# A fused retention and ELU feed-forward kernel on one core: w_out brought in by converting transfers on GpSimd's queue, and the second group's first matrix product cut in two halves

## The chip, the cores and the metric

The kernel runs on one core of a Trainium2 chip. The core has a tensor engine (TensorE, PE in the profile, with PEld for its weight loads), a vector engine (VectorE, DVE), a scalar engine (ScalarE, ACT), GpSimd (POOL) and a sync engine (SyncE, SP), which here only issues transfers. Each engine runs its own list of instructions in order, and they wait for each other by semaphores. Transfers between the chip's main memory and the core's working memory run on sixteen DMA engines, whichever engine issued them; those issued by SP and those issued by GpSimd stand in two different queues (q1 and q0 in the profile). The metric is the device time of one execution in microseconds, and the number given for a kernel is the median of several executions.

## The reference

Inputs and output are float32. The first part is a retention (attention with a decay in place of the softmax), the second a feed-forward network with an ELU between two matrix products.

```python
# q, k, v: [8 batches, 8 heads, 576 tokens, 64]; w_in: [512, 2048]; w_out: [2048, 512]
scores = (1 / sqrt(64)) * q @ k.transpose(0, 1, 3, 2)
gamma  = 1 - 2 ** (-5 - arange(8))                       # one decay for each head
Dmat   = where(rel >= 0, gamma ** rel, 0)                # rel = query position - key position
attn   = (scores * Dmat) @ v
x      = attn, heads side by side: [4608 tokens, 512]
h      = x @ w_in
g      = where(h > 0, h, exp(min(h, 0)) - 1)             # ELU
out    = g @ w_out                                       # [4608, 512]
```

## The kernel before

**Units.** The retention is cut into units, listed in `seq` (L161 to L166). A unit of a batch is a half `T` of its first 512 tokens (256 tokens) and a half `w` of the heads (four), so a batch has four such units, and one tail unit for its last 64 tokens with all heads. Units 0 to 3 are batch 0, units 4 to 7 batch 1, units 8 and 9 the tails of batches 0 and 1, units 10 to 13 batch 2, unit 14 its tail, and so on. The decay is a power of the position, so it is folded into q and k while they are converted to bf16 (`cast_qk`, L192): two instructions for q, two for k, one for v (`cast_v`). Then q and k are turned, either by a transposing transfer issued by SP (`turn`, L233) or on TensorE with a copy back by VectorE or ScalarE (`turn_pe`, L238). `stretch(u)` (L409) is the work of a unit on TensorE: the part of unit u-1 that comes from earlier tokens (`inter`), the scores of u, the masked scores of u-1 times v (`values`), and the running state of u (`state`). VectorE adds the state up (`prefix_mid`, `prefix_end`), and GpSimd copies it into block form for TensorE (`put_mid`, `put_end`, L403 and L406, two instructions each). `puts` does both copies, and `finish(u)` is the last half of a stretch alone. `put_x` lays the result down as the bf16 columns of the feed-forward input.

**Feed-forward.** The 4608 tokens make nine groups: group g below 8 is the first 512 tokens of batch g, and group 8 (`B` in the code, tiles `xtail` and `gt`) is the eight tails. For a group, `ffn1(g, ft)` (L460) is block ft of sixteen of the first product: four matmuls into a PSUM tile `ph`, an exponential and a relu on ScalarE, and one instruction on VectorE that makes the bf16 tile `g`. `ffn2(g, it, fts)` (L501) adds blocks of the second product for 128 tokens into `pm`; after block 15, ScalarE copies the result and GpSimd issues the store at the next `flush`. With `nf=2` and 256 columns, `ffn1` puts two blocks of half the tokens into one PSUM tile (used for group 8, `f1t`). There are three PSUM banks with the tag `ph`, one with `pm`, two for scores and two (`x0`, `x1`) for the retention's sums; the first group borrows the last two for some of its `ph` tiles (L649).

**Weights.** w_in and w_out come as float32 in sixteen pairs of 128-row blocks (`load_w(k)`, L150): eight pairs of w_in and eight of w_out, 256 KB a transfer, two transfers a pair, issued by SP into the ring of float32 tiles `rqk` (ten tiles), which the units' q and k use as well (`load`, L174). `cast_w(k)` (L155) converts a pair to bf16, two instructions on GpSimd. Block ft of the first product needs a quarter of w_in (two pairs), and row ft of the second product needs one block of w_out.

**Order.** Every instruction is pinned to the order in which the code issues it (`pin`). The order of the first third is written out by hand: loads of units 0 to 3 and of six weight pairs, the retention of batch 0 (L532 to L597), then group 0's two products woven with the remaining weight conversions and with units 4 to 7 (L632 to L709, where `one(ft, r)` is one block of the first product and row r of the second for the first two `it`). SP's list there is: pairs 4, 5, 10, 11, unit 4, pairs 6, 7, 12, 13, unit 5, pairs 14, 15, units 6, 7, 8, 10, 9. From L748 on, `stage(jobs, upto)` spreads unit steps evenly over feed-forward jobs. A step (L602) loads four units ahead, converts and turns two units ahead, and does the stretch of its own unit, so seven steps lie in the first stage (units 8 to 14) and five in most others.

## Time and profile before

| | |
|---|---|
| three runs | 317.7, 319.59 and 319.09 us, median 319.09 |
| the profiled execution's own time | 321.6 us |
| its span | 319.9 us |
| busy share of the span | PE 95%, ACT 66%, POOL 54%, DVE 52% |
| transfers | 54.00 MB, of them 8.92 MB in GpSimd's queue (q0), 44.58 MB in SP's (q1) |

How to read it: a time in a view is counted from the start of the span. A group of instructions carries the line of the code that made it, the engine, and the output and inputs by the program's names. "[1.50 <-DMA qkT<-qkn]" behind an instruction says how long its engine sat idle before it and what ended that. All matmuls have the line of the helper `mm` (L65), so they are told apart by their tiles. In the table by stretches of time, each row has the busy time of every engine, the clock that TensorE was granted (1.00 is full), the busy share of the sixteen DMA engines (which can exceed 1, since packets overlap) and the bytes per time that they moved.

### The profile page before, as it was taken

How to read it: one execution, taken by the hardware profiler on the slowest of the kernel's cores; microseconds unless marked ns; L12 is line 12 of the kernel's file. 1: busy time of each engine (PE TensorE's matmuls, PEld its weight loads, DVE VectorE, ACT ScalarE, POOL GpSimd, SP SyncE). 2: the span in 40 equal slices, each digit the busy share in tenths (PEclk: the TensorE clock that was granted, in tenths of full speed). 3: DMA queues.
4: the chain of work that ended last, by engine and by line, in shares of the span. 5: the costliest groups of instructions: out<-in, count | busy, mean ns of one | idle time of the engine just before them, and what ended most of it. 6: DMA issues, size and time to landing. Idle time of an engine off the chain costs nothing.

```text
span 319.9 us, 7923 instructions
## 1 busy us (share of the span) xinstructions
PE 304.4 (95%) x3104; PEld 158.1 (49%) x3104; DVE 166.8 (52%) x309; ACT 212.1 (66%) x417; POOL 173.9 (54%) x380
## 2 busy tenths in 40 slices
PE   8889698997999999999999999999999999999994
PEld 5544344543554544554444675545454544456541
DVE  5755557267756765654445564665456543434400
ACT  3678455576777886777677777677777777677511
POOL 5889867896697775646354555555965200001010
PEclk9799979999999999999999999999999999999998
DMA  7999999499999997658366464764943000000112
GB/s 214 316 329 360 355 290 242 126 261 224 204 232 279 252 214 210 170 148 181 102 164 174 142 166 118 164 182 133 216 99 85 35 33 33 35 33 34 60 74 66
DMA packets 100774, 54.00 MB, mean 169 GB/s; under 512 B 45056, under 2 KB 94208, under 8 KB 100736
## 3 DMA queue, kind: packets, MB, share of 16 engines
q1 hardware_dynamic: 97984, 44.58, 58.2%
q0 software_dynamic: 2752, 8.92, 7.8%
q8 instruction: 24, 0.39, 0.5%
q14 instruction: 14, 0.11, 0.1%
HBM read 36.70 MB, written 9.44 MB: 144 GB/s over the span
## 4 chain that ended last, share of the span: by engine, by line
PE 79%; POOL 7%; DMA 7%; ACT 2%; DVE 1%; issue 1%; SPq 1%; ACTq 0%; POOLq 0%
PE pm L65 36%; PE ph L65 34%; PE x L65 5%; PE sc L65 4%; DMA rqk<-in_k_dram 3%; POOL qkn L197 3%; DMA qkT<-qkn 2%; DMA rqk<-in_moe_w_in_dram 2%; POOL w_in_sb L158 2%; ACT e L470 1%; PE ptr L246 1%; POOL w_out_sb L158 1%; DVE g L481 1%; SPq L186 1%; POOL s_mid L401 0%
## 5 line engine op out<-in xcount | busy, mean ns | idle before, releaser
L481 DVE SCALAR_TENSOR_TENSOR g<-e,ph 128x512 bf16<-128x512 f32 x128 | 87.5, 686 | 106.4 <-ACT ph L474 106.2
L65 PE MATMUL ph<-xt,w_in_sb 128*128 128x512 bf16 x512 | 131.8, 382 | 1.8 <-DVE g L481 0.9
L65 PE MATMUL pm<-w_out_sb,g 128*128 128x512 bf16 x512 | 131.9, 380 | 0.7 <-POOL w_out_sb L158 0.4
L470 ACT ACTIVATE e<-ph 128x512 f32<-128x512 f32 x144 | 85.9, 596 | 57.2 <-PE ph L65 57.1
L65 PEld LDWEIGHTS <-w_in_sb 128*128 128x128 bf16 x640 | 60.3, 98 | 63.2 <-issue 3.8
L474 ACT ACTIVATE ph<-ph 128x512 f32<-128x512 f32 x144 | 85.2, 594 | 0.0
L65 PEld LDWEIGHTS <-g 128*128 128x128 bf16 x512 | 49.4, 98 | 57.0 <-issue 1.7
L518 POOL DMA_DIRECT2D out_dram<-ot x36 | 20.5, 570 | 82.3 <-ACT ot L509 75.6
L401 POOL CAST s_mid<-mid 64x128 bf16<-64x128 f32 x64 | 18.6, 291 | 41.9 <-DVE mid L385 21.2
L197 POOL TENSOR_TENSOR qkn<-rqk,gk 128x256 bf16<-128x256 f32 x64 | 38.0, 614 | 4.7 <-DMA rqk<-in_k_dram 4.5
L304 DVE TENSOR_TENSOR pt<-sc,mask 128x1024 bf16<-128x1024 f32 x31 | 37.8, 1218 | 3.1 <-PE sc L65 3.1
L359 ACT CAST xt<-x 128x256 bf16<-128x256 f32 x62 | 23.5, 450 | 15.8 <-PE x L65 15.6
L509 ACT COPY ot<-pm 128x512 f32<-128x512 f32 x36 | 20.9, 587 | 19.4 <-PE pm L65 19.4
L197 POOL TENSOR_TENSOR qkn<-rqk,gq 128x256 bf16<-128x256 f32 x50 | 29.6, 612 | 1.6 <-DMA rqk<-in_q_dram 0.2
L481 DVE SCALAR_TENSOR_TENSOR gt<-e,ph 128x256 bf16<-128x256 f32 x32 | 12.0, 417 | 14.9 <-ACT ph L474 14.9
L65 PE MATMUL sc<-qkT 64*64 64x128 bf16 (+1 forms) x576 | 16.0, 221 | 1.9 <-DMA qkT<-qkn 1.5
L65 PE MATMUL ph<-xtail,w_in_sb 128*128 128x256 bf16 x128 | 16.6, 273 | 0.0
L200 POOL CAST vn<-rv 128x512 bf16<-128x512 f32 x27 | 16.3, 605 | 0.0
L65 PE MATMUL pm<-w_out_sb,gt 128*128 128x512 bf16 x64 | 15.3, 379 | 0.0
L65 PEld LDWEIGHTS <-qkT 64*64 64x64 bf16 x576 | 9.9, 107 | 7.1 <-DMA qkT<-qkn 1.9
L65 PE MATMUL x<-pt,vn 64*64 64x128 bf16 x496 | 13.0, 220 | 0.0
L246 PE MATMUL ptr<-ident,qkn 128*128 128x128 bf16 x64 | 7.8, 243 | 4.1 <-POOL qkn L197 2.3
(71 smaller groups left out, 188.2 us busy)
## 6 DMA issues: line engine op xcount, KB each, us to landing
rqk<-in_q_dram SPq DMA_DIRECT2D x32, 256.0 KB, 3.9
rqk<-in_k_dram SPq DMA_DIRECT2D x32, 256.0 KB, 4.1
rv<-in_v_dram SPq DMA_DIRECT2D x32, 256.0 KB, 4.6
out_dram<-ot POOLq DMA_DIRECT2D x32, 256.0 KB, 2.5
rqk<-in_moe_w_in_dram SPq DMA_DIRECT2D x16, 256.0 KB, 5.9
rqk<-in_moe_w_out_dram SPq DMA_DIRECT2D x16, 256.0 KB, 5.9
rqt<-in_q_dram SPq DMA_DIRECT2D x8, 128.0 KB, 4.3
rqt<-in_k_dram SPq DMA_DIRECT2D x8, 128.0 KB, 4.1
```

The costliest lines, as they stand in the source:

```text
L65: pin(nc.tensor.matmul(*a, **kw))
L197: pin(tt[eng](natt[u][0][:, i, e], x[:, e], g[:, e], ALU.mult))
L200: pin(engines[eng](natt[u][1], rawt[u][1]))
L246: pin(nc.tensor.transpose(p[:, j], flat(u)[:, lo : lo + P], ident))
L304: pin(nc.vector.tensor_tensor(ptt[u].rearrange("p i h n -> p (i h) n"), sc.rearrange("p i (h n) -> p (i h) n", h=2), m.to_broadcast([P, 4, ...
L359: pin(engines[eng[c]](dst, src))
L401: pin(engines[eng](dst[half(i), :, half(i)], src[half(i)]))
L470: pin(nc.scalar.activation(e[:, :m], ph[:, :m], AF.Exp))
L474: pin(nc.scalar.activation(ph[:, :m], ph[:, :m], AF.Relu))
L481: pin(nc.vector.scalar_tensor_tensor(dst, e[:, c], -1.0, ph[:, c], ALU.add, ALU.min))
L509: pin(nc.scalar.copy(ot, pm))
L518: pin((queue or nc.gpsimd).dma_start(dst, src))
```

## The change

The eight pairs of w_out are no longer loaded by SP and converted by GpSimd. `ask_w(r)` issues, on GpSimd's queue, one transfer for two blocks of w_out (512 KB of float32 read) that writes bf16 straight into `w_out_sb`; there are eight of them, placed between GpSimd's conversions of w_in. w_in is loaded by SP into a ring of its own with the tag `rw` (four tiles), so the fifth to eighth pair each wait until the conversion of the pair four before them is done; units 4 to 7 then take the same four tiles, so that the load of unit 4 + i waits for the conversion of pair 4 + i. The ring `rqk` shrinks from ten tiles to six. SP's list becomes w_in pairs 0 to 7, units 4, 5, 6, 7, 8, 10, 9.

Group 0 runs six blocks of its first product ahead of its second (it was four), almost all of it comes before unit 4, and units 4 to 7 are turned on TensorE between row 11 and the third and fourth `it` of group 0. More of the conversion of their q and v goes to VectorE and ScalarE. Group 1's first product is made in two halves of 256 tokens (`f1h`): the first half, which needs only units 4 and 5, is woven into the end of group 0's second product; the second half goes into the first stage, beside `it` 0 and 1 of group 1's second product. The function `both` goes. Units 8, 9 and 10 are converted and turned ahead of the first stage, so its first step converts nothing.

```diff
--- before.py
+++ after.py
@@ -45,7 +45,7 @@
     assert (DM, S, D, HP) == (H * D, FT * P + ST, 64, KJ)
 
     const = ctx.enter_context(tc.tile_pool(name="const", bufs=1))
-    raw = ctx.enter_context(tc.tile_pool(name="raw", bufs=10))
+    raw = ctx.enter_context(tc.tile_pool(name="raw", bufs=6))
     nat = ctx.enter_context(tc.tile_pool(name="nat", bufs=4))
     tpool = ctx.enter_context(tc.tile_pool(name="tpool", bufs=4))
     ppool = ctx.enter_context(tc.tile_pool(name="ppool", bufs=2))
@@ -137,25 +137,23 @@
     tt = {"v": nc.vector.tensor_tensor, "p": nc.gpsimd.tensor_tensor}
     staged = {}
 
-    def weights(k):
-        for i in (2 * k, 2 * k + 1):
-            n, j = divmod(i, KJ)
-            if n < KJ:
-                c = slice(n * 512, (n + 1) * 512)
-                yield i % 2, moe_w_in[j * P : (j + 1) * P, c], w_in_sb[:, j, c]
-            else:
-                f = i - KJ * KJ
-                yield i % 2, moe_w_out[f * P : (f + 1) * P, :], w_out_sb[:, f, :]
-
     def load_w(k):
-        staged[k] = raw.tile([P, 2, 4, 2, D], FP32, name="rqk", tag="rqk").rearrange("p i h e d -> p i (h e d)")
-        for h, src, dst in weights(k):
-            pin(nc.sync.dma_start(staged[k][:, h], src))
+        n, j = divmod(2 * k, KJ)
+        c = slice(n * 512, (n + 1) * 512)
+        x = raw.tile([P, 2, 4, 2, D], FP32, name="rw", tag="rw", bufs=4).rearrange("p i h e d -> p i (h e d)")
+        staged[k] = [(x[:, h], w_in_sb[:, j + h, c]) for h in range(2)]
+        for h in range(2):
+            pin(nc.sync.dma_start(x[:, h], moe_w_in[(j + h) * P : (j + h + 1) * P, c]))
 
     def cast_w(k, eng="pp"):
-        for h, src, dst in weights(k):
+        for h, (src, dst) in enumerate(staged[k]):
             if eng[h] != " ":
-                pin(engines[eng[h]](dst, staged[k][:, h]))
+                pin(engines[eng[h]](dst, src))
+
+    def ask_w(r):
+
+        pin(nc.gpsimd.dma_start(w_out_sb[:, 2 * r : 2 * r + 2],
+                                moe_w_out[2 * r * P : (2 * r + 2) * P, :].rearrange("(f p) c -> p f c", p=P)))
 
 
     seq = []
@@ -171,7 +169,7 @@
     def is_tail(u):
         return seq[u][1] == 2
 
-    def load(u, last=False):
+    def load(u, last=False, **ring):
         b, T, w = seq[u]
         if is_tail(u):
             rqk = raw.tile([P, H, D], FP32, name="rqt", tag="rqt", bufs=2)
@@ -179,7 +177,7 @@
             for dst, src in ((rqk[:ST], q), (rqk[ST:], k), (rv, v)):
                 pin(nc.sync.dma_start(dst, src[b, :, FT * P :, :].rearrange("h p d -> p h d")))
         else:
-            rqk = raw.tile([P, 2, 4, 2, D], FP32, name="rqk", tag="rqk")
+            rqk = raw.tile([P, 2, 4, 2, D], FP32, name="rqk", **(ring or dict(tag="rqk")))
             rv = raw.tile([P, 4, 2, D], FP32, name="rv", tag="rv", bufs=6)
             parts = [(rqk[:, 0], q), (rqk[:, 1], k), (rv, v)]
             for dst, src in parts[2:] + parts[:2] if last else parts:
@@ -531,7 +529,7 @@
 
     for u in range(FT):
         load(u, last=u == FT - 1)
-    for kk in (0, 1, 2, 3, 8, 9):
+    for kk in range(6):
         load_w(kk)
     new_x()
     warm(7)
@@ -584,6 +582,7 @@
     put_x(2)
     drop(2)
     cast_w(1)
+    ask_w(0)
     banks = (st3, st)
     for hl in range(2):
         masks(3, (hl,))
@@ -592,9 +591,11 @@
         put_x(3, (hl,), banks[hl], ("ss", "sv")[hl])
     drop(3)
     cast_w(2)
+    ask_w(1)
+    cast_w(3)
+    ask_w(2)
     put_end(2)
     put_end(3)
-    cast_w(3)
 
     nxt = [8]
     loaded = [12]
@@ -608,8 +609,9 @@
         while loaded[0] <= min(u + 4, NS - 1):
             load(loaded[0])
             loaded[0] += 1
-        cast(u + 2)
-        turn(u + 2)
+        if u != 8:
+            cast(u + 2)
+            turn(u + 2)
         stretch(u)
 
     def f1(g):
@@ -617,8 +619,8 @@
             return []
         return [lambda ft=ft: ffn1(g, ft, kind=kind(ft), defer=True) for ft in range(NFT)]
 
-    def f1t(hf):
-        return [lambda ft=ft: ffn1(B, ft, hf * 256, 256, kind="r", nf=2, defer=True) for ft in range(0, NFT, 2)]
+    def f1h(g, hf):
+        return [lambda ft=ft: ffn1(g, ft, hf * 256, 256, kind="r", nf=2, defer=True) for ft in range(0, NFT, 2)]
 
     lasts = set()
 
@@ -629,15 +631,11 @@
 
 
 
-    for kk in (4, 5, 10, 11):
+    for kk in (6, 7):
         load_w(kk)
-    load(4)
-    for kk in (6, 7, 12, 13):
-        load_w(kk)
-    load(5)
-    for kk in (14, 15):
-        load_w(kk)
-    for u in (6, 7, 8, 10, 9):
+    for u in range(4, 8):
+        load(u, tag="rw", bufs=4)
+    for u in (8, 10, 9):
         load(u)
     F = {0: {}, 1: dict(pool=ps_h, tag="ph"), 2: {}, 3: dict(pool=ps_h, tag="ph")}
 
@@ -646,67 +644,88 @@
             ffn2(0, it, [ft], **F[it])
 
     def one(ft, r=None):
-        bank = dict(pool=ps_x, tag=f"x{ft // 2 % 2}") if ft % 2 and ft < 12 else {}
+        bank = dict(pool=ps_x, tag=f"x{ft // 2 % 2}") if ft % 2 and ft < 10 else {}
         ffn1(0, ft, kind="r", **bank)
         if r is not None:
             row(r)
 
     for ft in range(4):
         one(ft)
-    for kk in (8, 9, 4, 5, 10, 11):
-        cast_w(kk)
-    for ft in range(4, 8):
-        one(ft, ft - 4)
-    cast(4, "p", "p", "p")
-    for ft in range(8, 10):
-        one(ft, ft - 4)
-    for kk in (6, 7):
-        cast_w(kk)
-    for ft in range(10, 12):
-        one(ft, ft - 4)
-    turn_pe(4, "sv")
-    for kk in (12, 13):
-        cast_w(kk)
-    cast(5, None, "p", "p")
-    one(12, 8)
-    cast_qk(5, 0, "v")
+    for ft in range(4, 6):
+        one(ft)
+    cast_w(4)
+    ask_w(3)
+    cast_w(5)
+    ask_w(4)
+    for ft in range(6, 10):
+        one(ft, ft - 6)
+    ask_w(5)
+    cast_w(6)
+    ask_w(6)
+    ask_w(7)
+    cast_w(7)
+    one(10, 4)
+    one(11, 5)
+    row(6)
+    one(12, 7)
+    one(13, 8)
+    cast(4, "p", "p", "s")
+    row(9)
+    one(14, 10)
+    turn_pe(4, "vs")
+    one(15, 11)
+    row(12)
     stretch(4, None)
-    turn_pe(5, "sv")
-    one(13, 9)
-    one(14, 10)
-    puts(4)
-    stretch(5, None)
-    cast_w(14)
-    one(15, 11)
-    cast_w(15)
-    puts(5)
-    cast(6, "v", "p", "s")
-    row(12)
+    cast(5, "v", "p", "s")
     row(13)
     row(14)
     row(15)
+    puts(4)
+    cast(6, None, "p", None)
     flush()
-    turn_pe(6, "sv")
     ffn2(0, 2, Q[0])
-    cast(7, "v", "p", "s")
+    turn_pe(5, "vs")
+    ffn2(0, 2, Q[1])
+    stretch(5, None)
+    cast_qk(6, 0, "v")
+    cast_v(6, "s")
+    ffn2(0, 2, Q[2])
+    turn_pe(6, "vs")
+    cast(7, None, "p", None)
+    puts(5)
+    ffn2(0, 2, Q[3])
     stretch(6, None)
-    ffn2(0, 2, Q[1])
-    turn_pe(7, "sv")
-    puts(6)
+    cast_qk(7, 0, "v")
+    cast_v(7, "s")
     cast(8)
-    ffn2(0, 2, Q[2])
-    ffn2(0, 2, Q[3])
-    stretch(7, None)
-    ffn2(0, 3, Q[0], **F[3])
-    ffn2(0, 3, Q[1], **F[3])
-    puts(7)
-    finish(7)
-    ffn2(0, 3, Q[2], **F[3])
-    ffn2(0, 3, Q[3], **F[3])
-    cast(9)
     turn(8)
     load(11)
+    puts(6)
+    half1 = f1h(1, 0)
+
+    def some():
+        half1.pop(0)()
+        settle()
+
+    ffn2(0, 3, Q[0], **F[3])
+    some()
+    turn_pe(7, "sv")
+    some()
+    ffn2(0, 3, Q[1], **F[3])
+    stretch(7, None)
+    cast(9)
     turn(9)
+    flush()
+    some()
+    ffn2(0, 3, Q[2], **F[3])
+    puts(7)
+    cast(10)
+    turn(10)
+    some()
+    finish(7)
+    ffn2(0, 3, Q[3], **F[3])
+    while half1:
+        some()
     def mix(a, c):
 
         jobs, n = [], 0
@@ -736,24 +755,15 @@
 
     two = {g: f2(g, range(4)) for g in range(1, B)}
 
-    def both(g, lag=3):
-        def job(i):
-            if i < NFT:
-                ffn1(g, i, kind="r")
-            if i >= lag:
-                for it in range(2):
-                    ffn2(g, it, [i - lag], **F[it])
-        return [lambda i=i: job(i) for i in range(NFT + lag)]
-
-    stage(both(1), 15)
+    stage(mix(f1h(1, 1), f2(1, (0, 1))), 15)
     stage(mix(f1(2), f2(1, (2, 3))), 20)
     stage(mix(f1(3), two[2]), 25)
     stage(mix(f1(4), two[3]), 28)
-    stage(mix(f1t(0), two[4][:8]), 30)
+    stage(mix(f1h(B, 0), two[4][:8]), 30)
     stage(mix(f1(5), two[4][8:] + f2(B, (0, 1))), 35)
     stage(mix(f1(6), two[5]), 40)
     stage(mix(f1(7), two[6]), NS + 1)
-    for x in mix(f1t(1), two[7][:8]):
+    for x in mix(f1h(B, 1), two[7][:8]):
         run(x)
     settle()
     for n, (g, it) in enumerate([(7, 2), (7, 3), (B, 2), (B, 3)]):
```

## The prediction

> **What bounds the kernel now.** The page comes first: TensorE is busy nearly all the time, so the change can only win what TensorE stands idle or runs at a lowered clock.
>
> ```profile
> span 319.9 us, 7923 instructions
> ...
> PE 304.4 (95%) x3104; PEld 158.1 (49%) x3104; DVE 166.8 (52%) x309; ACT 212.1 (66%) x417; POOL 173.9 (54%) x380
> ```
>
> That leaves 15.5 us of idle in the whole span. Where it lies is read from the table by stretches. Its columns: stretch and length, then busy time and instructions of PE, PEld, DVE, ACT and POOL, the granted clock, the DMA engines' busy share, GB/s.
>
> ```profile
> 20.00:24.00 4.00, 4.00 (x19) 1.61 (x18) 1.70 (x4) 3.39 (x8) 3.77 (x10) 1.00 1.02 373
> 24.00:28.00 4.00, 3.83 (x19) 1.68 (x18) 2.52 (x4) 3.73 (x8) 4.00 (x8) 1.00 1.06 391
> 28.00:32.00 4.00, 4.00 (x20) 1.84 (x19) 2.06 (x3) 3.37 (x7) 3.59 (x7) 1.00 1.14 328
> 32.00:36.00 4.00, 3.30 (x21) 1.54 (x18) 2.40 (x4) 2.75 (x6) 4.00 (x8) 1.00 1.05 382
> 36.00:40.00 4.00, 1.96 (x40) 0.87 (x39) 1.70 (x4) 1.09 (x2) 2.64 (x6) 1.00 1.15 329
> 40.00:44.00 4.00, 3.27 (x13) 1.22 (x12) 1.72 (x4) 1.49 (x3) 3.77 (x9) 0.66 1.12 331
> 44.00:48.00 4.00, 4.00 (x64) 2.11 (x63) 2.29 (x3) 2.55 (x7) 1.23 (x3) 0.91 1.10 249
> ```
>
> Two readings. TensorE is idle for 0.17 + 0.70 + 2.04 + 0.73 = 3.64 us here, and the clock of 0.66 and 0.91 behind the longest gap costs another 0.34 x 3.27 + 0.09 x 4 = 1.5 us. And the DMA engines are full throughout (1.02 to 1.15): this stage, which brings in the weights and units 4 to 7, is held by transfers. The waits of TensorE (total, times, longest) and the chain name single places.
>
> ```profile
> PE ptr L246 <- POOL qkn L197: 2.3, 6, 0.8
> PE ptr L246 <- DVE qkn L197: 1.7, 1, 1.7
> ```
>
> ```profile
> 33.95 5.85 DMA rqk<-in_k_dram
> 39.87 1.20 POOL qkn L197 x2
> ...
> 70.51 5.85 DMA qkT<-qkn
> ...
> 298.77 0.86 PE pm L65 x4
> 299.63 0.87 PE ph L65 x8
> ```
>
> Transposes on TensorE wait for q and k to be converted; the chain shows one behind it, unit 5's k, asked for at 33.95 and landed at 39.8. Near 76 us the chain runs through a unit turned by a transfer.
>
> **The change, part by part.** The next fence shows TensorE's timeline where I need it: start, length, instructions.
>
> ```profile
> 19.58 4.56 PE L65 MATMUL ph<-xt,w_in_sb 128*128 128x512 bf16 x20
> ...
> 54.05 0.61 PE L246 MATMUL ptr<-ident,qkn 128*128 128x128 bf16 x8
> 54.50 1.89 PE L65 MATMUL pm<-w_out_sb,g 128*128 128x512 bf16 x8
> 56.23 0.28 PE L65 MATMUL x<-qkT,s_first 128*128 128x128 bf16 x2
> ...
> 57.24 1.90 PE L65 MATMUL pm<-w_out_sb,g 128*128 128x512 bf16 x8
> 58.98 0.27 PE L65 MATMUL x<-qkT,s_first 128*128 128x128 bf16 x2
> ...
> 59.76 1.90 PE L65 MATMUL pm<-w_out_sb,g 128*128 128x512 bf16 x8
> 61.50 1.89 PE L65 MATMUL ph<-xt,w_in_sb 128*128 128x512 bf16 x8
> ...
> 76.40 0.42 PE L65 MATMUL sc<-qkT 64*64 64x128 bf16 x16 [1.50 <-DMA qkT<-qkn]
> ```
>
> From start to start: turning a unit takes 54.50 - 54.05 = 0.45 us, a stretch 57.24 - 56.23 = 1.01, `finish` 59.76 - 58.98 = 0.78, four matmuls of 512 columns 0.86 to 0.87 (57.24 to 58.98 for eight).
>
> *The halves.* Eight matmuls of 256 columns take 0.87 where four of 512 take 0.86 (end of the chain): cutting costs TensorE 16 x 0.01 us, nothing. Moving eight such jobs, 8 x 0.87 = 6.96 us, ahead of the first stage gains nothing by itself: the same work would have been done later. So I compare the new start of the first stage with 61.50 + 6.96 = 68.46.
>
> *Fewer instructions on GpSimd, and the new requests.* Gone are sixteen conversions and sixteen issues by SP; new are eight requests on GpSimd. The conversions, the nearest requests (the stores), and a copy of a state into block form (two instructions):
>
> ```profile
> 18.33 2.85 POOL L158 CAST w_in_sb<-rqk 128x512 bf16<-128x512 f32 x5
> 51.18 1.27 POOL L518 DMA_DIRECT2D out_dram<-ot  x2
> 219.48 1.11 POOL L518 DMA_DIRECT2D out_dram<-ot  x2 [3.18 <-ACT ot L509]
> ...
> L518 POOL DMA_DIRECT2D out_dram<-ot x36 | 20.5, 570 | 82.3 <-ACT ot L509 75.6
> ...
> 73.91 0.64 POOL L401 CAST s_mid<-mid 64x128 bf16<-64x128 f32 x2 [2.21 <-DVE mid L385]
> ```
>
> A conversion takes 2.85 / 5 = 0.57, so 9.1 us go. A store of 256 KB takes 0.57; the pair at 219.48 are stores of half that size and take 0.56 each. A request of 512 KB should therefore cost between 0.56 and, were it in proportion to the bytes, 1.14; I take 0.57, since half the bytes saved nothing: 8 x 0.57 = 4.6 us. GpSimd is 4.5 us better off.
>
> A rule that speaks against this move: the Trainium skill, "SBUF — State Buffer", section "SBUF: two separate sides", in its box on the "DVE blocks DMA" trap, says that GpSimd cannot write descriptors while VectorE runs an instruction in a two-port mode. The pair at 51.18, beside VectorE work, took 1.27 against 1.11, so the trace bears out 0.08 us a request; by the rule a request could wait out a whole VectorE instruction, which is the rival "GpSimd late" below.
>
> *The transfers.* The bytes read stay the same, and the engines are full, so what counts is their order and the price of a converting transfer, which this trace does not show. Rows for the transfers:
>
> ```profile
> 41.62 1.92 SPq L186 DMA_DIRECT2D rqk<-in_k_dram  x1
> ...
> rqk<-in_k_dram SPq DMA_DIRECT2D x1, 256.0 KB, 7.0
> ...
> rqk<-in_moe_w_out_dram SPq DMA_DIRECT2D x16, 256.0 KB, 5.9
> qkT<-qkn SPq DMA_TRANSPOSE x24, 3.5
> ```
>
> The eight requests read 8 x 0.524 = 4.19 MB. At 356 GB/s, the mean of the six rows from 20 to 44, that is 11.8 us of full engines. A converting transfer might take half that, if only written bytes count (-5.9 us), or twice (+11.8). I take the price of a plain one: every plain transfer reads what it writes, and the reads do not change.
>
> Then unit 7's k, the last request at 41.62, landing 7.0 us later at 48.6, cannot come earlier than now, for the same bytes lie ahead of it. Nor need it come later, if requests keep coming. Each ring tile is freed by a conversion on GpSimd: from 18.33, fifteen conversions (8.6), eight requests (4.6) and two units' `put_end` (2 x 0.64 = 1.3) end at 32.8, or near 35 with an allowance for the last w_in pair, which shares the engines with three requests. So unit 7's k is asked for by 36, before its present 41.62.
>
> What waits for that k is new. `cast(7)` puts its conversion on GpSimd ahead of `puts(5)`, and `stretch(6)` begins with `inter(5)`, which needs `put_mid(5)`. GpSimd stands in its queue until 48.6, converts (1.20, the chain's row), copies the middle state (0.64): `stretch(6)` starts at 50.5. Is TensorE ready by then? From 19.58: sixteen blocks (13.8), sixteen rows of two matmuls (6.9), four quarters of `it` 2 (3.5), three turns (1.4), two stretches (2.0), together 27.5, ends at 47.1. So up to 3.4 us of smaller stalls are hidden: the block that first needs w_in's third quarter, whose conversions now come after three requests, rows 10 and 14 waiting for w_out, and unit 4's conversions behind the last w_in pair. The trace shows none of them; if they stay within 3.4 together they cost nothing, and that is the value I take.
>
> Behind 50.5 lie two stretches, a turn, four quarters of `it` 3, `finish` and the eight half jobs: 2.02 + 0.45 + 3.48 + 0.78 + 6.96 = 13.7, to 64.2. The last four half jobs follow each other, and there ScalarE is slower than TensorE:
>
> ```profile
> L470 ACT ACTIVATE e<-ph 128x512 f32<-128x512 f32 x144 | 85.9, 596 | 57.2 <-PE ph L65 57.1
> L481 DVE SCALAR_TENSOR_TENSOR gt<-e,ph 128x256 bf16<-128x256 f32 x32 | 12.0, 417 | 14.9 <-ACT ph L474 14.9
> ```
>
> Two activations are at most 1.19 a job against 0.87, so up to 1.3 us over four, nothing if the three banks absorb it; I take 0.6. VectorE's two instructions, 0.83, fit. That gives 64.8 against 68.46: 3.7 us gained.
>
> *The first stage.* It has the same seven steps over 16 jobs of 0.87 where there were 19 of 1.3, so a step comes every 1.74 + 1.0 = 2.7 us. GpSimd's work for a full step is longer, two state copies and the conversions in this fence:
>
> ```profile
> 75.33 1.18 POOL L197 TENSOR_TENSOR qkn<-rqk,gq 128x256 bf16<-128x256 f32 x2
> ...
> 77.60 0.61 POOL L200 CAST vn<-rv 128x512 bf16<-128x512 f32 x1
> ```
>
> Twice 0.64, twice 1.18 and 0.61 make 4.25. It starts with units 8 to 10 done, but from unit 13 on the path is: state of unit 10, copies (1.3), q and k (2.4), transfer that turns them (3.5 by the median, 5.85 in the chain's row), and about 1 us of VectorE before: 8.2 to 10.5 against three steps of 2.7 and so 8.1. A stall of 0.1 to 2.4 us, on average what the 1.50 at 76.40 is now. I count zero, and keep both ends for the range.
>
> **The sum.** The profiled execution took 321.6 with a span of 319.9; less 3.7 that is 317.9, with a span of 316.2. It is 2.5 above the median of 319.09, so against the median the forecast is 315.4.
>
> **Rivals.** *Converting transfers are cheap.* Nothing in the trace is for or against. If they take half, unit 7 lands 5.9 us earlier, and TensorE's own sum (47.1) binds: up to 3.4 more, less about 0.5 for smaller stalls, 312.5.
>
> *Converting transfers are dear (the other side).* If they take twice, 11.8 us fall on full engines ahead of unit 7, and the place is the same wait of `stretch(6)`: 315.4 + 11.8 = 327.2. It turns the gain into nothing at 3.7 / 11.8 = 31% dearer and into a loss of 1% at 58%. Against it: the present stores in GpSimd's queue run at 8.92 MB for 7.8% of the engines' time, the loads at 44.58 MB for 58.2%:
>
> ```profile
> q1 hardware_dynamic: 97984, 44.58, 58.2%
> q0 software_dynamic: 2752, 8.92, 7.8%
> ```
>
> so that queue is not slow in itself. The Trainium skill, "DMA: Bandwidth & Descriptors", section "Issuing engines are not separate DMA queues", has both queues on the same sixteen engines; full engines at 1.02 to 1.15 agree that a second queue adds no bandwidth.
>
> *GpSimd late, no change.* Priced at the dear end of its bounds, 1.14, a request costs 0.57 more and eight cost 4.6: the last w_in pair is ready at 39.6, and the middle of the thirteenth block waits for it. Behind that lie three and a half blocks (3.0), nine rows (3.9), three turns (1.4), two stretches (2.0) and four quarters (3.5), 13.8 us, so `stretch(6)` starts near 53.4, 2.9 late; a first stage at its bad end loses another 2.4 - 1.5 = 0.9. The 3.7 are gone: 319.2. For it speaks the pair at 51.18, against it the mean of 0.57.
>
> **How the numbers follow.** About 1%, 3.2 us, is what a measurement of this kernel can tell from no change: the three runs span 1.9. The forecast gets 0.50, with a range of its own of 313.5 to 317.5, of which 0.31 lies below 315.9 and 0.19 above. Cheap transfers get 0.20, all of it faster. GpSimd late gets 0.16: 0.03 faster, 0.12 the same, 0.01 slower. Dear transfers get 0.14: 0.13 slower, 0.01 the same. So faster 0.54, the same 0.32, slower 0.14. The range is 311.5 to 321.0: it holds the first three cases and leaves most of the dear one out.
>
> **What would show it.** Right: TensorE idles in several pieces of 1 us or less between 27 and 47, `stretch(6)` starts near 50.5 behind unit 7's k and GpSimd, `it` 0 of group 1's second product starts near 66, and the requests take near 0.57 each. Wrong: DMA engines below 0.9 before 44 (then requests ran dry, not bandwidth), w_out landing long after its row is due with full engines at far less than 356 GB/s (dear), requests of over 1 us (GpSimd late), or a wait of TensorE for a turned unit of over 2.4 us in the first stage.

## The result and the profile after

| | before | after |
|---|---|---|
| three runs, median | 319.09 us | 331.95 us (331.23 to 332.14) |
| ratio to before, 95% interval | | 1.0405 [1.0361, 1.045] |
| the profiled execution, its span | 321.6, 319.9 us | 331.95, 330.2 us |

The changed kernel is 4% slower; the forecast was 1% faster. The page of the changed kernel, first its busy times, then its transfers by queue (packets, MB, share of sixteen engines' span):

```profile
span 330.2 us, 8062 instructions
...
PE 307.9 (93%) x3168; PEld 165.5 (50%) x3168; DVE 167.9 (51%) x325; ACT 212.5 (64%) x419; POOL 169.4 (51%) x370
...
q1 hardware_dynamic: 95680, 40.38, 55.7%
q0 software_dynamic: 4928, 11.01, 11.2%
```

TensorE's busy time is up by 3.5 us, its idle time by 6.8 (22.3 against 15.5). A fixed point late enough to see where the time went lies in the second stage, the sixth block of group 2's first product, in TensorE's timeline before and then after:

```profile
98.16 1.02 PE L65 MATMUL ph<-xt,w_in_sb 128*128 128x512 bf16 x4 [0.23 <-DVE g L481]
```

```profile
108.50 1.02 PE L65 MATMUL ph<-xt,w_in_sb 128*128 128x512 bf16 x4 [0.22 <-DVE g L479]
```

It starts 10.34 later, and the spans differ by 10.3, so everything lies before it. The table by stretches of the changed kernel has the same columns as in the prediction:

```profile
20.00:24.00 4.00, 4.00 (x20) 1.60 (x19) 0.54 (x3) 2.22 (x7) 4.00 (x7) 0.50 0.62 168
...
36.00:40.00 4.00, 4.00 (x20) 1.85 (x19) 2.04 (x3) 2.59 (x6) 1.18 (x2) 1.00 1.20 216
40.00:44.00 4.00, 1.95 (x12) 0.89 (x10) 0.71 (x2) 0.89 (x2) 1.18 (x2) 1.00 1.17 271
44.00:48.00 4.00, 0.50 (x5) 0.49 (x5) 1.02 (x2) 1.60 (x3) 1.18 (x2) 0.60 0.92 260
48.00:52.00 4.00, 4.00 (x42) 1.48 (x41) 0.70 (x2) 2.20 (x4) 0.00 (x0) 0.54 1.03 254
```

Three things stand out. At 20 to 24 the DMA engines are busy for only 0.62 of the time (1.02 before). From 36 to 44 they are full, but move 216 and 271 GB/s where they moved 329 and 331; a part of that is only the way of counting, for a request that reads 512 KB and writes half of it is listed with 256.0 KB. And from 42 TensorE stands, with a clock of 0.60 and 0.54 during and behind that. TensorE's timeline names the places:

```profile
32.34 0.59 PE L65 MATMUL pm<-w_out_sb,g 128*128 128x512 bf16 x2 [1.03 <-DMA w_out_sb<-in_moe_w_out_dram]
...
47.50 0.59 PE L244 MATMUL ptr<-ident,qkn 128*128 128x128 bf16 x4 [5.46 <-DVE g L479]
...
59.01 0.93 PE L244 MATMUL ptr<-ident,qkn 128*128 128x128 bf16 x8 [0.99 <-DVE qkn L195]
...
60.65 0.28 PE L65 MATMUL x<-qkT,s_mid 128*128 128x128 bf16 x2
...
91.52 0.28 PE L65 MATMUL x<-qkT,s_mid 128*128 128x128 bf16 x2 [1.91 <-POOL s_mid L399]
```

The row at 60.65 is the start of `stretch(6)`, which the forecast had near 50.5. The longest wait, 5.46 us in the middle of unit 4's turning, is put down to VectorE's `g`. VectorE was not the cause, though; what it waited for shows on ScalarE's timeline, and behind that in the chain of waits:

```profile
45.13 0.62 ACT L198 CAST vn<-rv 128x512 bf16<-128x512 f32 x1 [4.24 <-DMA rv<-in_v_dram]
45.65 0.59 ACT L468 ACTIVATE e<-ph 128x512 f32<-128x512 f32 x1
46.14 0.59 ACT L472 ACTIVATE ph<-ph 128x512 f32<-128x512 f32 x1
```

```profile
29.03 16.08 DMA rv<-in_v_dram
```

`cast(4, "p", "p", "s")` stands ahead of `one(14, 10)` in the code. So ScalarE's conversion of unit 4's v is in its list ahead of the two activations of block 14. The v was on its way for 16.08 us; ScalarE stood for it, the activations behind it, VectorE's `g` behind them, and TensorE behind that (the turning takes its tiles from the same three banks as the blocks). Nobody needed v yet: `stretch(4)` uses it first, three jobs later.

Why v was late shows in SP's timeline (start, time in the issue) and SP's waits:

```profile
30.61 3.37 SPq L184 DMA_DIRECT2D rqk<-in_q_dram  x1
...
34.66 6.45 SPq L184 DMA_DIRECT2D rv<-in_v_dram  x1
...
46.58 0.79 SPq L184 DMA_DIRECT2D rqk<-in_k_dram  x1
```

```profile
SPq L146 <- POOL w_in_sb L151: 4.7, 4, 2.6
...
SPq L184 <- POOL w_in_sb L151: 4.0, 2, 2.2
```

SP waited 4.7 us for tiles of the ring of four before w_in pairs and 4.0 before units, so the engines ran empty first; then unit 4 came into the crowd of requests, and SP stood up to 6.45 us in a single issue. Unit 7's k, the last row of the first fence, was asked for at 46.58 and landed 5.6 us later. The prediction hung `stretch(6)` on it, but nothing waited for it. GpSimd came to its conversion only at 57.46, and the row shows no idle time before it:

```profile
57.46 1.20 POOL L195 TENSOR_TENSOR qkn<-rqk,gk 128x256 bf16<-128x256 f32 x2
```

### The profile page after: what moved, and what is told of

Its sections match the earlier page's. It is cut to its first block, busy times and chain, and to the rows that moved or that the text cites. A ratio compares the mean times of both kernels' runs of the same rounds, so it can differ in the third digit from the quotient of the medians.

```text
span 330.2 us, 8062 instructions
## 1 busy us (share of the span) xinstructions
PE 307.9 (93%) x3168; PEld 165.5 (50%) x3168; DVE 167.9 (51%) x325; ACT 212.5 (64%) x419; POOL 169.4 (51%) x370
## 4 chain that ended last, share of the span: by engine, by line
PE 78%; DMA 7%; POOL 5%; SPq 3%; ACT 3%; issue 2%; DVE 2%; POOLq 0%; ACTq 0%; DVEq 0%
PE pm L65 35%; PE ph L65 34%; PE x L65 5%; DMA rv<-in_v_dram 5%; PE sc L65 3%; SPq L184 3%; DMA rqk<-in_k_dram 2%; POOL w_in_sb L151 2%; POOL qkn L195 1%; DVE g L479 1%; ACT ph L472 1%; POOL s_mid L399 1%; PE ptr L244 1%; ACT e L468 1%; POOL w_out_sb L155 0%
## 5 line engine op out<-in xcount | busy, mean ns | idle before, releaser
L479 DVE SCALAR_TENSOR_TENSOR g<-e,ph 128x512 bf16<-128x512 f32 (+1 forms) x144 | 88.7, 627 | 112.7 <-ACT ph L472 112.5
L65 PE MATMUL ph<-xt,w_in_sb 128*128 128x512 bf16 (+1 forms) x576 | 133.7, 363 | 1.2 <-ACT xt L357 0.6
L65 PEld LDWEIGHTS <-w_in_sb 128*128 128x128 bf16 x704 | 67.0, 99 | 59.6 <-issue 4.7
L198 POOL CAST vn<-rv 128x512 bf16<-128x512 f32 x25 | 15.1, 603 | 0.0
## 6 DMA issues: line engine op xcount, KB each, us to landing
rqk<-in_q_dram SPq DMA_DIRECT2D x32, 256.0 KB, 3.8
rqk<-in_k_dram SPq DMA_DIRECT2D x32, 256.0 KB, 4.2
rv<-in_v_dram SPq DMA_DIRECT2D x32, 256.0 KB, 4.7
out_dram<-ot POOLq DMA_DIRECT2D x32, 256.0 KB, 2.9
rw<-in_moe_w_in_dram SPq DMA_DIRECT2D x16, 256.0 KB, 6.7
w_out_sb<-in_moe_w_out_dram POOLq DMA_DIRECT2D x8, 256.0 KB, 9.6
```

Of the source, the lines that this page charges most:

```text
L65: pin(nc.tensor.matmul(*a, **kw))
L198: pin(engines[eng](natt[u][1], rawt[u][1]))
L479: pin(nc.vector.scalar_tensor_tensor(dst, e[:, c], -1.0, ph[:, c], ALU.add, ALU.min))
```

## The experiments

Each ratio is to runs of the kernel before on the same chip, whose medians there are 319.75 to 320.52 (319.09 beside the first result), so a difference in us between kernels of two chips is uncertain by about 1.

**The wait of ScalarE.** Unit 4's v goes to GpSimd:

```diff
-    cast(4, "p", "p", "s")
+    cast(4, "p", "p", "p")
```

> The changed kernel with unit 4's v converted on GpSimd instead of ScalarE. Theory A (ScalarE stands in its queue on unit 4's v, which lands at 45.1 us, so block 14's activations and with them a bank for turning unit 4 come late): the 5.5 us gap of TensorE ahead of the second half of unit 4's transposes goes; a gap of 2 to 4 us comes at unit 4's state, where v is first needed, because v still lands near 45. 328 to 330.5 us. Theory B (the transfers themselves are late, whoever waits for them): the same time as the changed kernel, 331 to 333.

326.25 us, 1.0198 [1.0141, 1.0254] of before: 5.7 us less than after. The wait at the turning is 1.04 in place of 5.46, although v still took 15.5 us. That is below the range of theory A: the gap it expected at unit 4's state did not come.

**The ring.** Six staging tiles and not four:

```diff
-    raw = ctx.enter_context(tc.tile_pool(name="raw", bufs=6))
+    raw = ctx.enter_context(tc.tile_pool(name="raw", bufs=5))
...
-        x = raw.tile([P, 2, 4, 2, D], FP32, name="rw", tag="rw", bufs=4).rearrange("p i h e d -> p i (h e d)")
+        x = raw.tile([P, 2, 4, 2, D], FP32, name="rw", tag="rw", bufs=6).rearrange("p i h e d -> p i (h e d)")
...
-        load(u, tag="rw", bufs=4)
+        load(u, tag="rw", bufs=6)
```

> The changed kernel with six ring tiles for w_in instead of four (and five for the units' q and k instead of six), so that SP never waits for a conversion before the sixth pair is asked for. Theory B1 (the DMA engines ran dry between 18 and 24 us, busy shares 0.43 to 0.82, and what was lost there is late ever after): the share stays near 1 there, unit 4's v lands 2 to 3 us earlier, 328 to 330 us. Theory B2 (the requests on GpSimd's queue crowd out the units' transfers): unit 4's v still takes over 12 us from issue to landing, and the time stays within 1 us of 332.

324.11 us, 1.0122 [1.0066, 1.0179]: 7.8 less than after, the largest part of the loss and more than either theory expected. The engines are full from 18 on (1.05, 1.05 and 0.95 in stretches of 2 us), unit 4 is asked for 5.7 to 6.2 us earlier, and ScalarE converts v at 38.61 without a wait, though v took 15.1 us. The ring and ScalarE's place are two halves of one cause: either removes the gap.

**Unit 4 among the w_in pairs.**

```diff
-    for kk in range(6):
+    for kk in range(4):
         load_w(kk)
+    load(4)
+    for kk in range(4, 6):
+        load_w(kk)
...
-    for u in range(4, 8):
+    for u in range(5, 8):
```

> The changed kernel with unit 4 asked for ahead of the fifth and sixth w_in pairs, into a free tile of the units' ring, so before any request on GpSimd's queue. Theories B1 and B2 both: unit 4 lands by 25 us, the 5.5 us gap goes, the dry stretch is filled. B2 adds that unit 5, asked for among the requests, then is the late one, with over 10 us to landing. 325 to 328 us. Theory A alone gives the same gain for unit 4. If the time stays at 331 or above, none of them holds.

325.87 us, 1.0174 [1.0126, 1.0221]. The gap at the turning is 1.13. Unit 4's v now takes 6.9 us, and unit 5's, asked for among the requests in its place, 14.8. The first row of the second product waits 2.73 us for the first request of w_out, where the run with v on GpSimd waits 0.85 and 0.94 for the first two.

**Five requests and not eight, in the changed kernel.**

```diff
     def ask_w(r):
+        if r > 4:
+            return
...
-            mm(pm, gpart(g, ft, it * P, P), w_out_sb[:, ft], start=(ft == 0), stop=(ft == NFT - 1))
+            mm(pm, gpart(g, ft, it * P, P), w_out_sb[:, ft % 10], start=(ft == 0), stop=(ft == NFT - 1))
```

> The kernel after (331.95, its ring of four tiles and ScalarE's conversion of unit 4's v as they are) with only five of the eight converting requests; rows 10 to 15 of the second product use blocks 0 to 5 of w_out again, so that part of the result is left wrong. If the requests in flight are what keeps unit 4's v on its way for 16.1 us, so that ScalarE waits 4.24 us for it with the activations of block 14 behind it, v takes 10 us or less, the gap of 5.46 us before unit 4's turning shrinks below 1.5 and the time falls to 324 to 328. If the ring of four tiles alone makes unit 4 late, the gap stays at 4 or more and the time at 330 to 332.

325.81 us, 1.0166 [1.0132, 1.02]: 6.1 less than after. Unit 4's v is asked for at 29.34 (29.03 in the changed kernel), but lands after 10.4 us in place of 16.1, and the gap is 1.13. So the three requests, issued from about 30.5 to 33.7 in the changed kernel, are what made v late enough to matter. How much of that is their bytes and how much the price of converting, this run does not tell. The transfers of `rv`, from issue to landing, in the changed kernel and then in this one, and this one's gap:

```profile
DMA to landing us min/median/max: 3.8/4.7/16.1
```

```profile
DMA to landing us min/median/max: 3.6/4.7/10.4
```

```profile
42.93 0.38 PE L246 MATMUL ptr<-ident,qkn 128*128 128x128 bf16 x4 [1.13 <-DVE g L481]
```

**The same three requests taken from the kernel with six tiles and without the halves.** First that kernel, with `both(1)` put back as the first stage and the eight half jobs ahead of it gone:

```diff
-    half1 = f1h(1, 0)
...
-    stage(mix(f1h(1, 1), f2(1, (0, 1))), 15)
+    stage(both(1), 15)
```

> The changed kernel with six ring tiles and without the halves (group 1's first product whole, in the first stage beside the second, as before the change). If the two parts add up (the halves alone cost 3.8 us at the median, the changed kernel with six tiles 4.2): within 1.5 us of the kernel before, 319 to 321.5. If the halves were needed as cover for the new order: 323 or more.

321.63 us, 1.0053 [1.0018, 1.0088]: 2.5 less than with the halves. Then with five requests:

> The kernel with six staging tiles and without the halves (321.63), and only five of the eight converting requests; rows 10 to 15 of the second product use blocks 0 to 5 of w_out again, so that part of the result is left wrong. It takes 1.57 MB of reads away, about 6.6 us of full engines at the probe's 4.2 us per MB, which is what converting costs more than plain transfers would for all eight. If that surcharge is what holds units 4 to 7 there, unit 5 and the following land 4 to 6 us earlier and the time falls to 316 to 319. If the order of waits holds the stage and not the engines' work, it stays at 321 to 322.

321.5 us, 1.0033 [1.0003, 1.0063]: no difference. Unit 7's k is asked for at 37.51 in place of 42.89, and units 4 to 7 follow at the same pace. So with six tiles the last three requests hold nothing any more, dear or not; the first row still waits 1.81 us for the first one. What holds units 4 to 7 is shown by the chain of waits of this kernel between the scores of unit 5 and those of unit 6:

```profile
48.77 0.35 PE sc L65 x16
49.12 0.41 PE x L65 x32
49.53 0.75 ACT xt L359 x2
...
50.31 0.29 DVE mid L385
...
50.73 0.29 DVE end L394
51.02 1.03 DVE qkn L197 x2
...
52.09 0.51 PE ptr L246 x6
52.60 0.86 PE pm L65 x4
...
53.58 0.35 PE sc L65 x16
```

From `sc` to `sc` pass 4.81 us, one step behind the other: scores, VectorE's mask (1.23 us from 49.17, beside ScalarE's copy in the chain), states on VectorE, then the next unit's q behind them on VectorE (`cast_qk(6, 0, "v")` follows `stretch(5)` in the code), its turning, its scores. TensorE has 0.45 + 1.01 + 2 x 0.87 = 3.2 us of work for a unit, by the prediction's rows.

**Shortening that chain.** Unit 4 turned a block earlier and unit 6's q on GpSimd:

```diff
-    one(14, 10)
     turn_pe(4, "vs")
+    one(14, 10)
...
-    cast(6, None, "p", None)
+    cast(6, "p", "p", None)
-    cast_qk(6, 0, "v")
```

> The kernel of the line above, with unit 4 turned one block earlier (so that its transposes don't wait for the banks of blocks 13 and 14: 1.1 us in the trace with six tiles) and unit 6's q converted on GpSimd, which is idle there, instead of VectorE behind unit 5's masks (1.2 us). If these waits are on the path: 2 us less than without, 317 to 319.5. If transfers hold this stage anyway, the same time as without.

320.96 us, 1.0039 [1.0004, 1.0073]: 0.7 less, where 2 were expected; the intervals do not tell the two kernels apart. Then conversions ahead of the stretches as well:

```diff
+    cast(5, "p", "p", None)
     one(15, 11)
     row(12)
     stretch(4, None)
-    cast(5, "v", "p", "s")
+    cast_v(5, "s")
...
-    cast(7, None, "p", None)
     puts(5)
+    cast(7, "v", "p", None)
     ffn2(0, 2, Q[3])
     stretch(6, None)
-    cast_qk(7, 0, "v")
```

> The kernel with six staging tiles, without the halves, unit 4 turned a block earlier (320.96), with the conversions of q moved ahead: unit 5's on GpSimd ahead of the stretch of unit 4, unit 7's on VectorE ahead of the stretch of unit 6, and the copies of unit 5's states ahead of unit 7's conversion in GpSimd's list. If the stretches of units 4 to 7 now follow each other at the pace of mask, states, conversion and turning, one behind the other (4.7 us a unit, TensorE idle 1.33, 1.06 and smaller pieces), about 2 to 3 us go and the time falls to 318 to 319.5. If the transfers of the units still hold that stage, it stays at 320.5 to 322.

320.27 us, 0.9999 [0.9979, 1.002]: level with before, and between the two ranges. `stretch(6)` starts at 51.45, not far from the 50.5 forecast. Behind it TensorE now waits 0.86 and 1.78 us for state copies that stand behind conversions on GpSimd. So `puts(6)` and `puts(7)` went ahead of `cast(8)` and `cast(9)`:

> The kernel with the conversions ahead (320.27, ratio 0.9999 to before), and in GpSimd's list the copies of the states of units 6 and 7 ahead of the conversions of units 8 and 9. In its profile TensorE stands 0.86 and 1.78 us for these copies at 55.7 and 59.9, behind conversions, one of which waits 0.60 us for its own transfer. If GpSimd's order there is all that is left, about 2.5 us go: 317.5 to 318.5, under the kernel before. If something else is next (the transfer-turned unit 8, the blocks behind it), 319 to 320.5.

321.65 us, 1.0043 [1.0009, 1.0077]: a miss. The first step of the first stage does start at 61.53 in place of 63.32, but the next one then stands for unit 9's transposing transfer, where before has no wait:

```profile
65.81 0.25 PE L65 MATMUL sc<-qkT 64*64 64x64 bf16 x4 [1.58 <-DMA qkT<-qkt]
```

At 97.63 against 98.16 the profile has 0.5 us of the 1.8 left, and the medians show none. With the first row a block later as well:

> The same, and the first row of group 0's second product a block later (seven blocks of the first product ahead of it and not six), since TensorE stands 1.53 us at 26.2 for the first converting request. If that wait is on the path, 0.8 to 1.5 us less than the kernel with the copies first. If the turning of unit 4 behind it holds the stage anyway, no difference beyond 0.5 us.

321.83 us, 1.0051 [1.0017, 1.0085]. The first row waits 1.67 us for w_out all the same.

**The halves alone, in the kernel before.** `both(1)` replaced by the halves, eight half jobs woven into the end of group 0:

```diff
+    half1 = f1h(1, 0)
...
     ffn2(0, 3, Q[0], **F[3])
+    some()
+    some()
...
-    stage(both(1), 15)
+    stage(mix(f1h(1, 1), f2(1, (0, 1))), 15)
```

> The kernel before with only the second part of the change: group 1's first product in two halves, the first woven into the end of group 0's second product, units 8 to 10 converted ahead. The prediction's account (the halves gain nothing by themselves, the first stage's stall is what it was): 318 to 320.5 us. Theory C (a step every 2.7 us is too dense for GpSimd's 4.25, the changed kernel waited 0.58 and 1.91 us for state copies there): 320.5 to 323, with waits of TensorE for GpSimd's state copies in the first stage.

323.65 us, 1.011 [1.0083, 1.0138]. In its first stage TensorE waits 0.58 and 1.91 us for `s_mid`, to the digit as in the changed kernel. GpSimd's timeline in the changed kernel shows what is ahead of the copy:

```profile
88.01 1.17 POOL L195 TENSOR_TENSOR qkn<-rqk,gq 128x256 bf16<-128x256 f32 x2
89.15 1.17 POOL L195 TENSOR_TENSOR qkn<-rqk,gk 128x256 bf16<-128x256 f32 x2
90.28 0.60 POOL L198 CAST vn<-rv 128x512 bf16<-128x512 f32 x1
90.83 0.64 POOL L399 CAST s_mid<-mid 64x128 bf16<-64x128 f32 x2
```

Two tries to take the copies out of that list, on VectorE (the edit below) and on ScalarE (the same with `"s"`):

```diff
-        stretch(u)
+        stretch(u, "v" if u < 15 else "p")
```

> The kernel before with the halves alone (323.65), and in the first stage the copies of the states into block form on VectorE and not on GpSimd. If the halves lose because those copies stand behind conversions in GpSimd's list (0.58 and 1.91 us of waiting and the lowered clock behind it), TensorE waits there for at most 0.3 us and the time falls to 321 to 322, about 2 us. If the loss of the halves lies elsewhere, it stays at 323 to 324.

330.09 us, 1.0306 [1.0249, 1.0362], 6.4 us worse than the halves alone. VectorE's timeline, then GpSimd's (first and last row of a run of eleven instructions without a break of more than 0.1 us), then TensorE's:

```profile
79.18 0.47 DVE L401 CAST s_mid<-mid 64x128 bf16<-64x128 f32 x2
...
82.67 6.30 DVE L401 CAST s_mid<-mid 64x128 bf16<-64x128 f32 x2
```

```profile
81.92 1.18 POOL L197 TENSOR_TENSOR qkn<-rqk,gk 128x256 bf16<-128x256 f32 x2
...
87.58 0.60 POOL L200 CAST vn<-rv 128x512 bf16<-128x512 f32 x1
```

```profile
89.35 0.37 PE L65 MATMUL x<-qkT,s_mid 128*128 128x128 bf16 x2 [6.51 <-DVE end L394]
```

The same two copies take 0.47 us with GpSimd idle and 6.30 beside its conversions.

> The kernel before with the halves alone (323.65), and in the first stage the copies of the states into block form on ScalarE. With these copies on VectorE one pair of them took 6.30 us in place of 0.46 while GpSimd's conversions ran without a break, and TensorE stood 6.51 us. If that was the two engines keeping each other out, the copies on ScalarE take 0.3 us each beside the same conversions. If the halves lose because the copies stand behind conversions in GpSimd's list (0.58 and 1.91 us), TensorE then waits at most 0.5 us there and the time falls to 321 to 322.5. If the loss of the halves lies elsewhere, it stays at 323 to 325.

326.66 us, 1.0187 [1.0153, 1.0221]: worse by 3.0 than the halves alone (2.5 by the ratios), and the second wait is 2.22 in place of 1.91. The copies take 0.3 us each, but they stand on ScalarE ahead of the activations; those come later, with them VectorE's `g`, and the mask and state behind `g`. So GpSimd's list is not the whole reason. The step itself (two jobs of 0.87 and a stretch of 1.0) is shorter than the chain of scores, mask, state and copy, whichever engine copies. That is the reading that fits all three; a first stage with the halves and wider steps was not tried.

**The price of converting.** Transfers added to the changed kernel near its end, where the engines are nearly idle. The first probe let them run ahead of each other:

> The changed kernel with transfers added near its end, where the DMA engines are nearly idle, into tiles that nothing reads: two converting requests of 512 KB alone; two plain float32 requests of 512 KB on GpSimd's queue alone; six transfers of a unit's kind (256 KB, 512-byte rows) on SP's queue alone; six of a weight's kind (256 KB, 2 KB rows) alone; then two converting requests at once with the six unit transfers; the same with the six weight transfers; and two requests cut into four pieces each (512-byte rows read) at once with the six unit transfers. Theory 'dear': a converting request takes well over the plain one's time. Theory 'crowding by packets' (the two queues take turns by packets, so large packets on GpSimd's queue beat small ones on SP's): converting and plain cost about the same alone; beside the requests the unit transfers land at least twice as late as alone (by 3 us or more) while the weight transfers are held up less, by about the bytes that go between; beside the cut requests the units are held up less than beside the whole ones. Theory 'fair by bytes': unit and weight transfers are held up equally.

332.41 us. The pieces that were to coincide did not. Two converting requests, alone but for a store, landed after 5.3 us. The second probe ties them to stores:

> The kernel after with added transfers in the last stretch, tied to stores so that they start together: two converting requests of 512 KB alone (c_alone), two plain ones of the same rows and size alone (p_alone), two converting ones beside transfers of unit form (512-byte rows, s_conv) and beside transfers of weight form (2 KB rows, l_conv). If converting is what is dear, c_alone keeps the engines busy for about 4.4 us (their share summed over time) for its 1.05 MB, as in the probe before, and p_alone for about 2.8, a ratio near 1.55. If it is GpSimd's queue or the 512 KB form that is dear, p_alone takes 4 or more too. If rows of 512 bytes lose against the requests and rows of 2 KB do not, s_conv takes 8 us or more from issue to landing and l_conv 6 or less; if both only share the engines, the two land alike.

331.7 us. The first two fences are the windows of 8 and 7 us around the two converting and the two plain requests, each with one store of 128 KB in either queue; the last two hold the landings of converting requests beside rows of 512 bytes (`s_conv`) and of 2 KB (`l_conv`) on SP's queue:

```profile
q0 software_dynamic: 592, 0.66, 48.3%
q1 hardware_dynamic: 80, 0.13, 8.4%
...
c_alone<-in_moe_w_out_dram POOLq DMA_DIRECT2D x2, 256.0 KB, 4.3
```

```profile
q0 software_dynamic: 336, 1.18, 43.9%
q1 hardware_dynamic: 80, 0.13, 9.3%
...
p_alone<-in_moe_w_out_dram POOLq DMA_DIRECT2D x2, 512.0 KB, 4.5
```

```profile
s_conv<-in_q_dram SPq DMA_DIRECT2D x2, 256.0 KB, 6.5
c_small<-in_moe_w_out_dram POOLq DMA_DIRECT2D x2, 256.0 KB, 8.1
s_conv<-in_k_dram SPq DMA_DIRECT2D x2, 256.0 KB, 9.0
```

```profile
l_conv<-in_moe_w_out_dram SPq DMA_DIRECT2D x4, 256.0 KB, 7.3
c_large<-in_moe_w_out_dram POOLq DMA_DIRECT2D x2, 256.0 KB, 8.7
```

Less a store of the same size as q1's, two converting requests keep the engines busy for 0.483 x 8 - 0.67 = 3.19 us, two plain ones for 0.439 x 7 - 0.65 = 2.42. Converting is 32% dearer in these two windows, one pair of each, which makes 3.1 us for all eight by estimate; the ratio near 1.55 that was expected had counted a store of 256 KB in. The landings do not tell the row sizes apart clearly (6.5 to 9.0 against 7.3): that rows of 512 bytes lose against the requests is not shown.

**A version of the kernel before.** Unit 5's load ahead of pairs 12 and 13, to remove the longest gap of before:

```diff
-    for kk in (6, 7, 12, 13):
+    for kk in (6, 7):
         load_w(kk)
     load(5)
-    for kk in (14, 15):
+    for kk in (12, 13, 14, 15):
...
```

The edit also puts unit 5's conversions on GpSimd ahead of those of pairs 12 and 13, and rows 8 to 10 a block later.

> The kernel before with unit 5's load ahead of weight pairs 12 and 13, and rows 8, 9 and 10 of the second product one block later. In the profile of before TensorE stands 2.4 us between 39.5 and 41 for unit 5 and loses about 1.5 us to the clock behind it. If the order of the transfers is what made that wait, the time falls to 316 to 318. If the engines are full and the wait only moves to the rows of w_out or to unit 6, it stays at 319 to 321.

321.9 us, 1.0043 [1.0011, 1.0075]: a miss. Unit 5 landed in time, and the gap is 1.76 as it was 1.70: the conversion of its q stands on VectorE behind block 12's `g`, which waits 1.69 us for ScalarE. Transfers and VectorE's list had ended there within 0.64 us of each other, so taking one away left the other.

No kernel tried here beats before; the nearest is level with it.

## Why the prediction was wrong

By medians the loss comes apart into steps that were undone one after the other: six tiles 7.8, the halves 2.5, and 1.75 for the rest of the order (321.63 against 319.88), 12.1 together against a loss of 12.9. Against the forecast's own marks, `stretch(6)` is 10.2 us late (60.65 against 50.5), `it` 0 of group 1's second product 12.2 (78.22 against 66), and the row at 108.50 is 14.0 later than 98.16 less the 3.7 that were to be won. So the step that failed lies mainly ahead of `stretch(6)`.

- *"Up to 3.4 us of smaller stalls are hidden."* Failed, and here is most of the loss. The wait that came last was to be for unit 7's k. What came last was ScalarE's wait for unit 4's v. Unit 4's conversions were looked for on GpSimd, behind the last w_in pair; the one on ScalarE, ahead of block 14's activations, was in the diff and was not weighed. It made a single stall of 5.46 us, and the clock of 0.54 behind it costs another (1 - 0.54) x 4 = 1.8. From the first block at 20.73 to `stretch(6)` TensorE stands idle for 39.92 - 31.75 = 8.2 us in all.
- *"Nor need it come later, if requests keep coming"; "unit 7's k is asked for by 36."* Failed, though this path did not come to bind. The step took the ring tile's conversion as the only thing SP waits for. The conversions did end near 35 as worked out (the last row starts at 33.73 and takes 1.37), yet k was asked for at 46.58. SP waited 8.7 us for the ring of four, all of it by 28.02, the engines ran at 0.62, and afterwards SP stood up to 6.45 us in an issue. With six tiles k is still asked for only at 42.89, and at 37.51 with five requests as well: the ring and the requests in flight both delayed it. The sign that was named for this (engines below 0.9 before 44) is there, at 20 to 24.
- *"Ends at 47.1"*, TensorE's own sum. Failed even with five requests and six tiles: `stretch(6)` starts at 53.30. From the first block at 19.71 TensorE is busy for 28.46 us, near the 27.5 of the sum, and idle for 5.1: 1.81 for the first w_out request, 1.13 for the banks at unit 4's turning, 1.23 for unit 6's q, and smaller pieces. The sum added up TensorE's work and left out these waits, above all the chain through VectorE, 4.81 us a unit against 3.2.
- *"I take the price of a plain one."* Mis-sized: 1.32, almost the 31% at which the prediction had nothing left. But the place was another. Where the ring has six tiles, three requests fewer win nothing, while in the changed kernel they win 6.1: what a request costs depends on whether anything waits for a transfer behind it. What the price of converting alone does to the kernel's time was not tried.
- *"I count zero"* for the first stage. Mis-sized: waits of 0.58 and 1.91, a clock of 0.58 behind them at 92 to 96 in the changed kernel, 2.5 to 3.8 us by medians for the halves as a whole. The reason given, steps of 2.7 us, was right; the wait named for it, a transfer that turns a unit, was not the one that came last.
- *The halves cost TensorE nothing*: right for the matmuls. *A request costs 0.57*: 0.71 to 0.90 in the trace, within its bounds. *GpSimd late*: did not happen; GpSimd itself stood 3.00 and 2.35 us for unit 4's q and k.

Of the rivals none was what came: the dear one had the price, but its mechanism alone gives about 319 at 31%.

## What to carry to other kernels

A conversion put on an engine that works in order is also a wait for its transfer, placed ahead of everything behind it in that list; ask of each moved conversion what stands behind it, as was done here for GpSimd and not for ScalarE. A ring that serves two kinds of loads holds the issuing queue at its tightest point and delays all that stands behind: unit 4 was asked for at 28.02 with four tiles and at 21.81 with six. More tiles do not thin out the crowd of transfers, though: unit 4's v took 16.1 and 15.1 us. Where units are handed on from engine to engine, the pace is the length of that chain and not one engine's sum: work it out as a chain.

## What the runs showed of the hardware

- VectorE's copies from f32 to bf16 in the working memory stood for 6.30 us beside GpSimd's conversions (0.47 without them), through about ten GpSimd instructions in a row. The Trainium skill, "SBUF — State Buffer", section "SBUF: two separate sides", has GpSimd and, in some of its modes, VectorE share a pair of ports by an exclusive lock that is held for a whole instruction while the other blocks. The trace agrees (on ScalarE the same copies took 0.3 us each beside the same conversions), and shows the loser waiting much longer than one instruction.
- In the one pair of windows of the probe a converting transfer cost 32% more engine time than a plain one of the same bytes read, though alone both land after 4.3 to 4.5 us.
- The clock of 20 to 24 was 0.50 in the changed kernel's profile and 1.00 in that with five requests, whose program is the same up to there; the latter had its 0.50 earlier, around 10 to 16. The first row of the second product starts at 28.56 and 28.14 in the two, so the low clock cost the changed kernel at most about 0.4 us by that row. Nothing here explains where such a stretch falls.
